# 1/z turned by VectorE, a rearranged beginning and end, ScalarE scaling of the values, and more tiles transposed by DMA in an attention-and-gate kernel

## The chip, the cores and the metric

The kernel runs on one core of a Trainium2 chip. A core has five engines that run their own instruction streams in order: TensorE (PE in the profile; PEld is its loading of weights), VectorE (DVE), ScalarE (ACT), GpSimd (POOL) and SyncE (SP), which here issues every DMA. They wait for one another only by semaphores. SBUF holds the working data, 128 partitions wide; PSUM is the memory that TensorE writes, in eight banks of 512 float32 for each partition. GpSimd does not reach PSUM. The metric is the device time of one execution in microseconds (us), lower being better.

## What is computed

An attention over pooled keys, and then a gated mixture along the rows of its result. Cut to what matters:

```python
# q: (4, 12288, 128), kv: (4, 384, 32, 128), all float32
kv_pool = kv.reshape(B, H // 4, 4, W // 4, 4, C).mean(axis=(2, 4))
k = v = kv_pool.reshape(B, -1, C) @ w_sr          # 768 keys of 128 channels
s = (q @ k.transpose(0, 2, 1)) / np.sqrt(C)
a = np.exp(s - s.max(-1, keepdims=True))
a /= a.sum(-1, keepdims=True) + 1e-09
x = a @ v                                         # (4, 12288, 128)
gate_pre = sum(conv_w[k] * xp[:, k:k + S, :] for k in range(5))   # xp: x behind 4 zero rows
out = (1 / (1 + np.exp(-gate_pre)) * (x @ w_val)) @ w_out
```

`w_val`, `conv_w` and `w_out` come as float64; the kernel takes their words and makes float32 of them on the chip.

## The kernel before

The work is cut into 96 groups of 512 queries, 24 for each of the four batches; a group has four tiles of 128 queries (`NT`), j = 0 to 3. For precision the scores are made of three products of high and low parts (`kh`, `kl`, `qh`, `ql`), and so is the attention's result (`vh`, `vl` with a high and a low float16 half of the probabilities).

A tile goes like this. `score` (L251) makes 128 x 768 scores with six matmuls into a pair of PSUM banks, `s`; there are three such pairs, so the scores of a tile have to wait until the tile three before it has left its pair. `row_max` (L257, VectorE) takes the row's maximum, `expo` (L269, ScalarE) the exponential with the row's sum into a column of `z`, `p_hi` (L316, ScalarE) the high half and `p_lo` (L320, VectorE) the low half, which is the last reader of `s`. The probabilities must be transposed before they can be multiplied with the values. That is done in one of two ways. With `j < g.by_dma` the two halves go to `hl` in SBUF, and DMA transposes (L324) bring them to `pt`, two tiles in one DMA or one tile by itself. Otherwise TensorE turns the tile (`turn`, L299, six transposes against the identity) back into its own bank pair ahead of `p_hi`. `by_dma` is 3, so that tile 3 is turned by TensorE; in the last batch it is 4 in every second group.

A group's later steps follow in later groups: 1/z one group later, the product with the values (`av_part`, L333, 18 matmuls in four portions) and `x` (`g_x`, L350, VectorE) two groups later, the convolution's products and sums (L360, L369, GpSimd, and one product L358 on ScalarE) three groups later, `val`, the gate and `out` (L389, L394, L399, L409) four groups later. The product with `w_val`, the product with `w_out`, the turned z and the setup of keys and values share the one bank `m`.

The order on each engine is written out by hand: `tc.manual_schedule()` keeps the program's order, and the loop over t (L470) issues, for tile t, the scores of tile t + 1, then this tile's steps, then the `p_lo` of tile t - 1. So at j = 0 VectorE takes the maximum of tile 0 and then the low half of tile 3 of the group before; `g_x` stands at the end of j = 3.

1/z: `norm_eps` adds 1e-9 on ScalarE at the group's end; in the next group VectorE takes the reciprocal of the four columns (L276, j = 0), TensorE turns the 128 x 128 tile `z` into `m` (L279), VectorE copies the four rows out (L286, j = 1), a DMA stores them to DRAM (`rd<-r`, L287), and another reads them back into every partition (`rb<-rd`, L292, j = 3).

Keys of the next batch are loaded in 16 pieces (`kvt`, L117), one step in each group; VectorE pools them (L120), TensorE projects them (L133), ScalarE writes `kh` and `vt`, VectorE `kl`. `column_scale` finds a power of two for each channel of the values in six small steps (`trickle`, two in each iteration) and makes `diag`, the identity times it; `values` (L176) multiplies `vt` with `diag`, which turns and scales the values at once.

The beginning (L434 to L461) loads and pools the first batch's keys in 16 pieces, projects them in halves and makes the first scores. The 14 small VectorE steps that make float32 of the weights (L89, L93, L96) drip into the first groups. The end (L539 to L592) finishes the last five groups, n5 to n1.

## Time and profile before

| | us |
|---|---|
| median of three runs (their range) | 1077.52 (1075.18 to 1078.14) |
| the profiled execution's own time | 1078.68 |
| its span in the trace | 1076.9 |
| busy in the span: PE, VectorE, ScalarE, GpSimd | 1038.4, 919.5, 903.7, 865.2 |
| span before the first row maximum | 28.25 |
| span behind the last group's sum of z | 26.5 |

The profile is that of one execution. Its page gives the busy time of each engine, a row of digits for each engine along the span, the chain of work that ended last, followed back from the last instruction, and the costliest groups of instructions. The timeline gives instructions of an engine in order of time, neighbours of one kind merged ("x2"), with the idle time before them in brackets and what ended it. TensorE's matmuls are pipelined and their ends are modelled, so starts are to be compared, not ends. "Frame" below means the time from one group's `norm_eps` (L273) to the next one's.

### The profile page before, as it was taken

Reading aid. Unit: us, or ns where it says so; the run is one execution under the profiler, and the core shown is the slowest. Engines: PE = TensorE matmul, PEld = TensorE weight load, DVE = VectorE, ACT = ScalarE, POOL = GpSimd, SP = SyncE. Lnnn points to the kernel's source line nnn. Section 1 sums busy time; section 2 is a strip of 40 time slices with the busy share of each in tenths; the row PEclk is TensorE's granted clock in tenths of the full one; section 3 lists DMA queues with packets and bytes.
Section 4 is the critical chain, followed back from the end, with each engine's and each line's share of the span. In section 5 each row is a group of like instructions: output and inputs, shape, how many; then the busy total and the mean of one; then the engine's idle time right before and its main releaser. Section 6 shows DMA issues by size and latency. Waiting matters only on the chain.

```text
span 1076.9 us, 16475 instructions
## 1 busy us (share of the span) xinstructions
PE 1038.4 (96%) x5102; PEld 706.5 (66%) x5102; DVE 919.5 (85%) x1290; ACT 903.7 (84%) x1659; POOL 865.2 (80%) x948
## 2 busy tenths in 40 slices
PE   1899999999999999999999999999999999999996
PEld 0666666666666666666676666666666666666663
DVE  6888989898888898988888989898888888888885
ACT  1788888888888888888888888888888988888882
POOL 0178888888888888888888888888887888888882
PEclk9999999999999999999999999999999999999999
DMA  7699999998889999999689999997899999999994
GB/s 285 115 237 215 214 225 234 200 192 190 182 186 234 226 222 224 220 214 188 156 182 221 248 216 219 235 218 177 174 203 191 200 209 218 206 194 212 201 178 120
DMA packets 505527, 220.25 MB, mean 205 GB/s; under 512 B 471520, under 2 KB 472288, under 8 KB 505440
## 3 DMA queue, kind: packets, MB, share of 16 engines
q1 hardware_dynamic: 505440, 219.20, 92.7%
q8 instruction: 41, 0.67, 0.2%
q14 instruction: 46, 0.38, 0.1%
HBM read 75.83 MB, written 25.36 MB: 94 GB/s over the span
## 4 chain that ended last, share of the span: by engine, by line
PE 89%; DVE 5%; ACT 2%; DMA 2%; issue 1%; POOL 0%; SPq 0%; DVEq 0%; ACTq 0%
PE s L251 36%; PE av L333 32%; PE m L389 7%; PE m L399 7%; PE s L299 5%; DMA kvt<-in_kv 2%; DVE nm L257 1%; PE m L279 1%; ACT s L269 1%; ACT hl L316 1%; DVE hl L320 1%; DVE pt L320 1%; DVE pool L120 0%; DVE x L350 0%; PE m L176 0%
## 5 line engine op out<-in xcount | busy, mean ns | idle before, releaser
L333 PE MATMUL av<-pt,vh 128*128 128x512 f16 x1140 | 387.1, 381 | 0.0
L369 POOL TENSOR_TENSOR sum<-sum,tap 128x512 f32<-128x512 f32 x282 | 360.3, 1278 | 22.1
L257 DVE TENSOR_REDUCE nm<-s 128x1 f32<-128x768 f32 x384 | 363.9, 948 | 2.8 <-PE s L251 2.8
L269 ACT ACTIVATE s<-s,nm 128x768 f32<-128x768 f32 x300 | 262.0, 873 | 88.7 <-DVE nm L257 80.0
L360 POOL TENSOR_SCALAR tap<-x,wm 128x512 f32<-128x512 f32 x376 | 253.4, 693 | 78.1 <-DVE x L350 76.8
L320 DVE SCALAR_TENSOR_TENSOR hl<-s,hl 128x768 f16<-128x768 f32 x300 | 284.8, 949 | 21.4 <-ACT hl L316 21.1
L251 PE MATMUL s<-kh,qh 128*128 128x384 f32 x768 | 252.9, 410 | 6.0 <-DVE hl L320 2.3
L316 ACT ACTIVATE hl<-s 128x768 f16<-128x768 f32 x300 | 243.0, 810 | 9.1
L333 PEld LDWEIGHTS <-vh 128*128 128x128 f16 x1164 | 113.5, 98 | 173.6 <-issue 81.5
L333 PE MATMUL av<-pt,vl 128*128 128x512 f16 x570 | 216.0, 379 | 0.0
L251 PE MATMUL s<-kh,ql 128*128 128x384 f32 x768 | 198.0, 339 | 0.0
L251 PE MATMUL s<-kl,qh 128*128 128x384 f32 x768 | 197.7, 338 | 0.0
L237 POOL TENSOR_TENSOR ql<-q,qh 128x512 fp32r<-128x512 f32 x96 | 122.0, 1271 | 93.3 <-ACT qh L233 92.5
L251 PEld LDWEIGHTS s<-kh,qh 128*128 128x128 f32 x768 | 132.4, 192 | 51.1 <-PE m L279 4.4
L251 PEld LDWEIGHTS s<-kl,qh 128*128 128x128 f32 x768 | 140.5, 189 | 0.5 <-DVE kl L146 0.5
L251 PEld LDWEIGHTS s<-kh,ql 128*128 128x128 f32 x768 | 139.8, 189 | 0.0
L394 DVE SCALAR_TENSOR_TENSOR h<-th,m 128x512 f32<-128x512 f32 x94 | 64.7, 688 | 69.0 <-PE m L389 63.4
L369 POOL TENSOR_TENSOR sum<-tap,tap 128x512 f32<-128x512 f32 x94 | 120.3, 1280 | 0.0
L350 DVE SCALAR_TENSOR_TENSOR x<-av,down,rb 128x512 f32<-128x512 f32 x95 | 71.3, 751 | 44.5 <-POOL ql L237 30.5
L333 PEld LDWEIGHTS <-vl 128*128 128x128 f16 x582 | 57.2, 98 | 76.6 <-issue 53.6
L399 PE MATMUL m<-h,wm 128*128 128x512 f32 x188 | 96.8, 597 | 1.2 <-DVE h L394 1.2
L389 PE MATMUL m<-x,wm 128*128 128x512 f32 x188 | 96.1, 592 | 0.0
(68 smaller groups left out, 1001.9 us busy)
## 6 DMA issues: line engine op xcount, KB each, us to landing
kvt<-in_kv SPq DMA_DIRECT2D x64, 384.0 KB
rb<-rd SPq DMA_DIRECT2D x96, 256.0 KB
q<-in_q SPq DMA_DIRECT2D x47, 512.0 KB
out<-o SPq DMA_DIRECT2D x46, 512.0 KB
pt<-hl SPq DMA_TRANSPOSE x192
rd<-r SPq DMA_DIRECT2D x96, 2.0 KB
out<-o SPq DMA_DIRECT2D x3, 256.0 KB
q<-in_q SPq DMA_DIRECT2D x2, 256.0 KB
```

The costliest lines, as they stand in the source:

```text
L237: nc.gpsimd.tensor_tensor(out=g.ql, in0=g.q, in1=g.qh.bitcast(F32), op=ALU.subtract)
L251: nc.tensor.matmul(s[:, h, :HALF], a[:, sl], k[:, h * HALF:(h + 1) * HALF], start=(i == 0), stop=(i == 2))
L257: nc.vector.tensor_reduce(out=nm, in_=g.s[j], axis=AX.XY, op=ALU.max, negate=True)
L269: nc.scalar.activation(out=halves(g.pf[j]) if on_pe(g, j) else g.s[j], in_=g.s[j], func=AF.Exp, bias=g.nm.pop(j), accum_out=g.z[:, j:j + 1])
L316: nc.scalar.activation(out=part(g, j, 0), in_=g.s[j], func=AF.Copy, scale=2.0 ** 15)
L320: nc.vector.scalar_tensor_tensor(out=part(g, j, 1), in0=g.s.pop(j), scalar=2.0 ** 15, in1=part(g, j, 0), op0=ALU.mult, op1=ALU.subtract)
L333: nc.tensor.matmul(out, g.st[v][:, k * P:(k + 1) * P], g.pt[:, j0:j1, a * NCH + k], start=(i == 0), stop=(i == len(AV_ORDER) - 1))
L350: nc.vector.scalar_tensor_tensor(out=g.x[:, HALO + c0:HALO + c1], in0=av, scalar=g.st["down"], in1=g.rb[:, c0:c1], op0=ALU.mult, op1=ALU.mult)
L360: eng.tensor_scalar(out=g.tap[k], in0=src, scalar1=w, scalar2=1.0, op0=ALU.mult, op1=ALU.mult)
L369: nc.gpsimd.tensor_tensor(out=s, in0=acc, in1=g.tap[k], op=ALU.add)
L389: nc.tensor.matmul(m, wval, g.x[:, HALO + c0:HALO + c1], start=True, stop=True)
L399: nc.tensor.matmul(m, wout, h, start=True, stop=True)
```

## The change

The parts, by what they do:

- 1/z: the reciprocal moves behind the low half of tile 3. VectorE then turns `z`, now 128 x 32, in four 32 x 32 transposes, and the store is issued there, still at j = 0. TensorE's transpose of `z` and VectorE's copy out of `m` are gone. `norm_rows`, the read back, moves from the end of j = 3 to j = 2.
- Transposes: tile 3 goes by DMA (`by_dma` 4) in every second group of the last batch, as before, and in the first three batches in groups 0, 18, 20 and 22, which load no keys: 12 groups more.
- Values: ScalarE scales `vt` in place by a column of powers of two, and `values` only transposes it against the identity. The VectorE step that made `diag` is gone.
- Beginning: the weights are loaded first, and their 14 VectorE steps run there; GpSimd pools six of the 16 pieces in four halvings each; the keys are projected in pieces of 384, 288 and 96 columns; the scores of the first three tiles are made in two halves, the first of them ahead of the last pieces.
- End: the products for n2 and n1 stand one behind the other, the last groups' convolutions have two of five products on ScalarE (`conv_mixed` in place of `conv_dve`), and the order of the rest is new.

```diff
-    zs = [const.tile([P, P], F32, name=f"z{i}") for i in range(3)]
+    zs = [const.tile([P, BLOCK], F32, name=f"z{i}") for i in range(3)]
...
-            lambda: v.tensor_scalar_mul(out=st["diag"], in0=ident, scalar1=up.bitcast(F32)),
+            lambda: nc.scalar.activation(out=st["vt"], in_=st["vt"], func=AF.Copy,
+                                         scale=up.bitcast(F32)),
...
-            nc.tensor.matmul(m[:, j * P:(j + 1) * P], st["vt"][:, k:k + P], st["diag"],
-                             start=True, stop=True)
+            nc.tensor.transpose(m[:, j * P:(j + 1) * P], st["vt"][:, k:k + P], ident)
...
-    def norm_turn(g, m):
-        nc.tensor.transpose(m[:, :P], g.z, ident)
-        g.rm = m[:NT, :P]
+    def norm_turn(g):
+        g.r = small.tile([BLOCK, P], F32, name="r")
+        for i in range(0, P, BLOCK):
+            nc.vector.transpose(out=g.r[:, i:i + BLOCK], in_=g.z[i:i + BLOCK])
...
-            g.by_dma = 4 if b == B - 1 and i % 2 == 0 else 3
+            g.by_dma = 4 if i % 2 == 0 and (b == B - 1 or not 0 < i <= PIECES + 1) else 3
...
+    convert = load_moe()
     for i in range(AHEAD):
         load_kv(0, st, i)
...
+    by_pool = (1, 3, 5, 7, 9, 11)
+    ends = {PIECES // 2: slice(0, HALF), PIECES - 2: slice(HALF, NK - 2 * PC),
+            PIECES: slice(NK - 2 * PC, NK)}
+    for step in convert:
+        step()
+    for i in range(1, PIECES + 1):
+        if i - 1 + AHEAD < PIECES:
+            load_kv(0, st, i - 1 + AHEAD)
+        (pool_halving if i in by_pool else pool_kv)(st, i - 1)
...
+        if i == PIECES - 3:
+            for j in first:
+                score(at(0), j, (0,))
...
-            score(nxt, (j + 1) % NT)
+            score(nxt, (j + 1) % NT, (1,) if t + 1 in first else range(2))
...
-        if last and j == 0:
-            norm_reciprocal(last)
-        if last and j == 1:
-            norm_store(last)
+        if last and j == 2:
+            norm_rows(last)
         drip()
         if prev:
             p_lo(prev, (j - 1) % NT)
...
         if last and j == 0:
-            norm_turn(last, misc())
+            norm_reciprocal(last)
+            norm_turn(last)
+            norm_store(last)
...
-        if last and j == 3:
-            norm_rows(last)
...
+    for i in range(NT):
+        av_part(n2, i)
...
+    avs = pair_of(half)
+    av_range(n1, avs[0], 0, len(AV_ORDER), 0, NT // 2)
     n4.m = g_val(n4, misc())
+    av_range(n1, avs[1], 0, len(AV_ORDER), NT // 2, NT)
     new_x(n2, n3, nc.scalar.copy)
     g_x(n2, n2.av)
+    gate2 = conv_mixed(n2, 0, GQ)
...
+    g_x(n1, avs[0], *cuts[0])
     h4 = g_h(n4.th, n4.m)
...
+    gates = [conv_mixed(n1, *cuts[0])]
...
+    g_x(n1, avs[1], *cuts[1])
...
+    gates.append(conv_mixed(n1, *cuts[1]))
```

What the change moves on an engine is best seen where the streams themselves are listed, by line, operation and tiles (the numbers at the names tell buffers of one name apart). First VectorE in one group of the first batch, from `x` to `h`. Before:

```order
L350 SCALAR_TENSOR_TENSOR x_1481<-av_1366,down_214,rb_1355 128x512
L257 TENSOR_REDUCE nm_1503<-s_1451 128x1
L276 RECIPROCAL z1_102<-z1_102 128x4
L320 SCALAR_TENSOR_TENSOR pt_1445<-s_1428,pt_1445 128x768
L257 TENSOR_REDUCE nm_1525<-s_1488 128x1
L286 COPY r_1531<-m_1512 4x128
L320 SCALAR_TENSOR_TENSOR hl_1506<-s_1451,hl_1506 128x768
L394 SCALAR_TENSOR_TENSOR h_1536<-th_1508,m_1521 128x512
```

The same stretch after the change:

```order
L363 SCALAR_TENSOR_TENSOR x_1652<-av_1538,down_273,rb_1487 128x512
L270 TENSOR_REDUCE nm_1672<-s_1623 128x1
L333 SCALAR_TENSOR_TENSOR pt_1617<-s_1598,pt_1617 128x768
L289 RECIPROCAL z2_103<-z2_103 128x4
L295 STREAM_TRANSPOSE r_1681<-z2_103 32x32 x4
L270 TENSOR_REDUCE nm_1700<-s_1657 128x1
L333 SCALAR_TENSOR_TENSOR hl_1675<-s_1623,hl_1675 128x768
L418 SCALAR_TENSOR_TENSOR h_1707<-th_1677,m_1696 128x512
```

The low half of tile 3 (`pt<-s,pt`) stands one place earlier, the reciprocal behind it, and four transposes come between it and the maximum of tile 1; the copy ahead of the low half of tile 0 (`hl<-s,hl`) is gone.

Second SyncE's queue over two groups of the last batch, the first with seven tiles' worth of transposes between two stores of 1/z. Before:

```order
L324 DMA_TRANSPOSE pt_11049<-hl_10981 128x24x128
L287 DMA rd_11126<-r_11125 4x128
L324 DMA_TRANSPOSE pt_11165<-hl_11099 128x24x128
L324 DMA_TRANSPOSE pt_11165<-hl_11099 128x12x128
L292 DMA rb_11202<-rd_11126 128x512
L413 DMA out_0<-o_11072 128x1024
L287 DMA rd_11249<-r_11248 4x128
```

After:

```order
L337 DMA_TRANSPOSE pt_11090<-hl_11019 128x24x128 x2
L300 DMA rd_11150<-r_11145 4x128
L305 DMA rb_11204<-rd_11150 128x512
L337 DMA_TRANSPOSE pt_11207<-hl_11138 128x24x128
L337 DMA_TRANSPOSE pt_11207<-hl_11138 128x12x128
L300 DMA rd_11273<-r_11268 4x128
L437 DMA out_0<-o_11113 128x1024
```

The read back `rb<-rd` now stands right behind the store that it reads, and ahead of the next group's transposes instead of behind them.

Third ScalarE in group 22 of the first batch, after the change (before, the same stretch has no operation on `vt`):

```order
L282 ACTIVATE s_2957,z1_102<-s_2957,nm_3009 128x2x384
L329 ACTIVATE hl_2941<-s_2957 128x768
L180 ACTIVATE vt_511<-vt_511,up_2921 128x768
L245 CAST qh_3020<-q_2739 128x512
L282 ACTIVATE s_2997,z1_102<-s_2997,nm_3037 128x2x384
```

The scaling of all 768 columns of `vt` comes between the high half of tile 2 and the exponential of tile 3.

## Rows read from the trace of the kernel before

**Rows 1.** From the page: the busy time of each engine with its share of the span and its instructions, and the share of each engine in the chain that ended last.

```profile
PE 1038.4 (96%) x5102; PEld 706.5 (66%) x5102; DVE 919.5 (85%) x1290; ACT 903.7 (84%) x1659; POOL 865.2 (80%) x948
...
PE 89%; DVE 5%; ACT 2%; DMA 2%; issue 1%; POOL 0%; SPq 0%; DVEq 0%; ACTq 0%
```

**Rows 2.** The timeline of ScalarE at the `norm_eps` of some groups: start, duration, instruction. In order: groups 19, 21, 23, 24 and 25 (the first batch's end and the second's beginning), then 78, 79 and 80 of the last batch.

```profile
237.13 0.21 ACT L273 ACTIVATE z<-z 128x4 f32<-128x4 f32 x1
...
259.69 0.21 ACT L273 ACTIVATE z<-z 128x4 f32<-128x4 f32 x1
...
281.62 0.20 ACT L273 ACTIVATE z<-z 128x4 f32<-128x4 f32 x1
...
292.23 0.21 ACT L273 ACTIVATE z<-z 128x4 f32<-128x4 f32 x1
...
303.55 0.20 ACT L273 ACTIVATE z<-z 128x4 f32<-128x4 f32 x1
...
873.20 0.20 ACT L273 ACTIVATE z<-z 128x4 f32<-128x4 f32 x1
...
883.49 0.20 ACT L273 ACTIVATE z<-z 128x4 f32<-128x4 f32 x1
...
894.10 0.20 ACT L273 ACTIVATE z<-z 128x4 f32<-128x4 f32 x1
```

**Rows 3.** The timeline of TensorE in the frame behind group 79, whose tile 3 it turns itself: the six transposes, the end of a portion of `av`, the transpose of z, the scores of the next tile; then the end of another portion and the scores behind it.

```profile
883.66 0.82 PE L299 MATMUL s<-ident,pf 128*128 128x128 f32 x6
...
886.46 0.59 PE L333 MATMUL av<-pt,vh 128*128 128x512 f16 x2
886.89 0.27 PE L279 MATMUL m<-ident,z 128*128 128x128 f32 x1
...
887.35 0.51 PE L251 MATMUL s<-kl,qh 128*128 128x384 f32 x2
...
889.13 0.38 PE L333 MATMUL av<-pt,vh 128*128 128x512 f16 x1
...
889.70 0.51 PE L251 MATMUL s<-kl,qh 128*128 128x384 f32 x2
```

**Rows 4.** The timeline of VectorE in the same frame; in brackets the idle time before an instruction and what ended it.

```profile
883.93 0.75 DVE L350 SCALAR_TENSOR_TENSOR x<-av,down,rb 128x512 f32<-128x512 f32 x1 [0.88 <-POOL ql L237]
...
885.46 0.17 DVE L276 RECIPROCAL z<-z 128x4 f32<-128x4 f32 x1
885.54 0.93 DVE L320 SCALAR_TENSOR_TENSOR pt<-s,pt 128x768 f16<-128x768 f32 x1
886.39 0.95 DVE L257 TENSOR_REDUCE nm<-s 128x1 f32<-128x768 f32 x1
887.25 0.27 DVE L286 COPY r<-m 4x128 f32<-4x128 f32 x1
887.45 0.95 DVE L320 SCALAR_TENSOR_TENSOR hl<-s,hl 128x768 f16<-128x768 f32 x1
```

**Rows 5.** The timeline in the frame behind group 78, whose tile 3 went by DMA: the low half of tile 3 on VectorE, the idle time of TensorE's weight load (PEld) and the scores behind it.

```profile
875.25 0.93 DVE L320 SCALAR_TENSOR_TENSOR hl<-s,hl 128x768 f16<-128x768 f32 x1
...
876.29 0.30 PEld L251 LDWEIGHTS s<-kh,qh 128*128 128x128 f32 x2 [0.40 <-PE m L279]
...
876.75 0.34 PE L251 MATMUL s<-kl,qh 128*128 128x384 f32 x1
```

**Rows 6.** Groups of instructions by line and shape: count, busy us, mean ns of one, idle time before them.

```profile
L176 PE MATMUL m<-diag,vt 128*128 128x128 f32 x48 | 6.9, 280 | 0.4 <-ACT o L409 0.4
...
L188 DVE TENSOR_TENSOR vl<-m,vh 128x384 f16<-128x384 f32 x8 | 4.4, 546 | 0.0
```

**Rows 7.** The timeline of VectorE in the frame behind group 21, where the steps of the column scale drip in: a step on one column, and the next maximum.

```profile
263.44 0.14 DVE L164 TENSOR_SCALAR pw<-big 128x1 int32<-128x1 int32 x1
263.50 0.95 DVE L257 TENSOR_REDUCE nm<-s 128x1 f32<-128x768 f32 x1
```

**Rows 8.** The timeline of ScalarE later in the same frame: an operation on 128 x 768 out of PSUM into SBUF.

```profile
269.81 0.91 ACT L269 ACTIVATE pf<-s,nm 128x768 f32<-128x768 f32 x1
```

**Rows 9.** The timeline of the beginning: the last piece's pooling, the second half's projection, the first row maximum.

```profile
22.67 0.95 DVE L120 TENSOR_REDUCE pool<-kvt 128x48 f32<-128x768 f32 x1 [0.80 <-DMA kvt<-in_kv]
23.68 1.65 PE L133 MATMUL s<-pool,wsr 128*128 128x384 f32 x2 [7.82 <-DVE pool L120]
...
28.25 0.96 DVE L257 TENSOR_REDUCE nm<-s 128x1 f32<-128x768 f32 x1 [1.42 <-PE s L251]
```

**Rows 10.** The timeline of the end: the read back of 1/z for the last group but one, the store of the last, the last product with the values for the last group but one, the last read back, `x` of the last group but one, a chain of four dependent steps of its convolution, the last `h`.

```profile
1053.73 0.84 SPq L292 DMA_DIRECT2D rb<-rd  x1
...
1054.63 0.32 SPq L287 DMA_DIRECT2D rd<-r  x1
...
1054.93 0.38 PE L333 MATMUL av<-pt,vh 128*128 128x512 f16 x1
...
1057.19 0.32 SPq L292 DMA_DIRECT2D rb<-rd  x1
1058.01 0.75 DVE L350 SCALAR_TENSOR_TENSOR x<-av,down,rb 128x512 f32<-128x512 f32 x1 [4.73 <-POOL sum L369]
...
1059.79 3.11 DVE L377 SCALAR_TENSOR_TENSOR fast<-x,wm,fast 128x512 f32<-128x512 f32 x4
...
1072.53 0.42 DVE L394 SCALAR_TENSOR_TENSOR h<-th,s 128x256 f32<-128x256 f32 x1 [0.15 <-ACT th L385]
```

More of the change, by code (lines that the diff above doesn't have):

```diff
@@ L18 @@
 GQ = 512
+BLOCK = 32
 NT = GQ // P
@@ L122, in pool_kv, with pool_halving @@
                                 axis=AX.X, op=ALU.add)
+    def pool_halving(st, i):
+        t = st.pop(("kv", i)).rearrange("c (k s) -> c k s", s=RR)
+        n = RR // 2
+        while n:
+            if n == 1:
+                to = st["pool"][:, i * PC:(i + 1) * PC].rearrange("c (k s) -> c k s", s=1)
+            else:
+                to = kvp.tile([C, PC, n], F32, name=f"half{n}", bufs=1)
+            nc.gpsimd.tensor_tensor(out=to, in0=t[:, :, :n], in1=t[:, :, n:2 * n], op=ALU.add)
+            t, n = to, n // 2
     def key_tiles(st):
@@ L211, in setup_steps @@
         steps = [lambda i=i: piece(i) for i in range(PIECES + 1)]
-        steps += [lambda h=h: project(st, h, misc()) or split_keys(st, h) for h in range(2)]
+        steps += [lambda sl=sl: project(st, sl, misc()) or split_keys(st, sl)
+                  for sl in (slice(0, HALF), slice(HALF, NK))]
         return steps + value_steps(st)
@@ L371, in g_conv, with conv_mixed, product @@
         g.gate = acc
-    def conv_dve(g, c0=0, c1=GQ):
+    def conv_mixed(g, c0, c1):
+        def product(k):
+            t = work.tile([C, GQ], F32, name=f"tap{k}", bufs=1 if k < TAPS - 1 else 2)
+            t = t[:, :c1 - c0]
+            nc.scalar.activation(out=t, in_=g.x[:, k + c0:k + c1], func=AF.Copy,
+                                 scale=cwt[:, k:k + 1])
+            return t
+        late = [product(k) for k in range(TAPS - 2, TAPS)]
         s = work.tile([C, GQ], F32, name="fast")[:, :c1 - c0]
         nc.vector.tensor_scalar_mul(out=s, in0=g.x[:, c0:c1], scalar1=cwt[:, 0:1])
-        for k in range(1, TAPS):
+        for k in range(1, TAPS - 2):
             nc.vector.scalar_tensor_tensor(out=s, in0=g.x[:, k + c0:k + c1],
@@ L379, in conv_dve @@
                                            op0=ALU.mult, op1=ALU.add)
+        for t in late:
+            nc.vector.tensor_tensor(out=s, in0=s, in1=t, op=ALU.add)
         return s
@@ L439, in attn_moe_kernel @@
     nc.sync.dma_start(out=wsr, in_=w_sr)
-    g_qh(at(0))
-    g_ql(at(0))
+    first = range(3)
+    by_pool = (1, 3, 5, 7, 9, 11)
+    ends = {PIECES // 2: slice(0, HALF), PIECES - 2: slice(HALF, NK - 2 * PC),
+            PIECES: slice(NK - 2 * PC, NK)}
     low = None
-    for i in range(PIECES):
-        if i + AHEAD < PIECES:
-            load_kv(0, st, i + AHEAD)
-        if i == 3:
-            convert = load_moe()
-        pool_kv(st, i)
-        if i == 3 * PIECES // 4:
+    for step in convert:
[4 more added lines that the diff above has]
+        (pool_halving if i in by_pool else pool_kv)(st, i - 1)
+        if i == PIECES // 2:
+            g_qh(at(0))
+            g_ql(at(0))
+        if low and (i == PIECES - 1 or i == PIECES - 3):
             low()
-        if i % (PIECES // 2) == PIECES // 2 - 1:
-            h = 2 * i // PIECES
-            project(st, h, bank_pair()[:, 0])
-            high, low = split_keys(st, h)
+            low = None
+        if i in ends:
+            project(st, ends[i], misc())
+            high, low = split_keys(st, ends[i])
             high()
+        if i == PIECES - 3:
+            for j in first:
+                score(at(0), j, (0,))
     low()
@@ L458, in attn_moe_kernel @@
     load_pair(at(2), at(3))
-    score(at(0), 0)
+    score(at(0), 0, (1,))
     g_qh(at(1))
```

83 lines of the change are left out of this document (35 added, 48 removed).

## The prediction

> **What bounds the kernel now.** I read the page first, then the frames between groups, then TensorE and VectorE inside a frame, then the two ends. TensorE is busy for 96% of the span and is 89% of the chain that ended last [rows 1], so in the middle a TensorE instruction less is time less, as long as nothing else is nearly as late. The frames say how near that is. Behind group 79, whose tile 3 TensorE turns itself, a frame takes 894.10 - 883.49 = 10.61 us; behind group 78, whose tile 3 went by DMA, it takes 10.29 [rows 2]. The six transposes hold TensorE for about 0.64 us (six at a pitch of 0.11, [rows 3]), but only 0.32 came back. Why is seen one step further: the low half of tile 3 ends at 876.18, TensorE's weight load sits idle for 0.40 us and starts 0.11 after that end [rows 5]. The page puts this idle time down to TensorE's own z transpose, but the bank pair's last reader is the low half, so I take VectorE as the releaser. So a closed loop lies right behind TensorE: `av` ends, VectorE makes `x`, the maximum of tile 0, the low half of tile 3, the maximum of tile 1, the low half of tile 0, and only then is a bank pair free for the scores of tile 3. The change takes work from TensorE and puts some on this loop, so the question is which of the two ends last.
>
> **1/z, TensorE's side.** From the last `av` start (886.46 plus a pitch of 0.21) to the `kl` scores it is 0.68 us with the z transpose between them and 0.57 without [rows 3]. TensorE saves 0.11 in each frame; a frame that it alone bounds falls from 10.61 to 10.50.
>
> **1/z, VectorE's side.** I lay the new order into the frame behind group 79 [rows 4]. The low half of tile 3 takes the reciprocal's place and runs from 885.46 to 886.39. Independent instructions overlap by 0.08 (the maximum at 886.39 starts before the low half ends at 886.47), so the reciprocal runs from 886.31 to 886.48. The four transposes of 32 x 32 are new, and no row shows one. From below: a step on one column adds only 0.06 between two large ones (263.44 to 263.50, [rows 7]), with 31 columns more about 0.10. From above: the copy of 128 columns took 0.27 [rows 4]. The nearest row is the one-column step, 0.14; between it and the maximum of 768 columns, 0.95, a column costs about 0.0011, so 32 columns are about 0.17. I take them one behind the other, since each has another group of partitions as input and they share the unit's transposing path, with the 0.03 that dependent steps show (four of 0.75 in 3.11 us, [rows 10]): a pitch of 0.20. That ends them at 886.50 + 3 x 0.20 + 0.17 = 887.27. The maximum of tile 1 then runs from 887.19 to 888.14 and the low half of tile 0 from 888.16 to 889.11; it ends now at 888.40. TensorE's `kl` scores for tile 3 stand at 889.70 and could stand at 889.59 without the z transpose. They follow the end of the low half by 0.57 behind group 78 [rows 5], and by 0.51 where VectorE is less crowded, so they come at 889.62 to 889.68: 0.03 to 0.09 late. **The frame becomes 10.50 + 0.05 = 10.55**, bound by VectorE, whether tile 3 goes by DMA or not. What was cover is used up: 0.70 us more on the loop, against some 0.65 that it had to spare.
>
> The Trainium skill (VectorE: DVE Perf Modes, Two Vector instructions with no wait between them) states that an instruction whose input starts in another group of 32 partitions than the last one's is held until all earlier ones have finished. No run here shows it; by it the four transposes are serial as I take them, and the overlapped case below falls away.
>
> **The store and the read back.** The store has its data at about 887.3 instead of 887.5. The read back now waits for it in SyncE's queue, with the next tiles' transposes behind it. How long that is shows at the end, where nothing else is queued: the last store's issue is over at 1054.95 and its read back starts at 1057.19, 2.2 us later [rows 10]. In most groups the store now has the time until the next transposes are ready; behind a group that goes all by DMA it is issued late, and delays the next transposes by those 2.2 us. Their product with the values is two groups away, so I cost it at nothing. If that cover were gone, each such group would pay up to 2.2 us.
>
> **More tiles by DMA.** In 12 frames TensorE loses 0.64 us, but VectorE's loop is the same 10.55, so they gain what the others gain. For the 11 such frames of the last batch, now 10.29, the loop is a loss of 0.26 each.
>
> **The sum of the middle.** 53 regular frames of the first three batches: 53 x -0.06 = -3.2. Two project frames a batch, now 11.28 each (237.13 to 259.69, [rows 2]): TensorE 11.17 in the first; in the second, whose tile goes by DMA, VectorE's 10.55 + 0.46 (one more split on 384 columns, 0.55 less the overlap, [rows 6]) = 11.01; together 3 x (-0.11 - 0.27) = -1.1. Two frames with `values`, now 11.32 (292.23 to 303.55): three of the six passes go (48 passes in 24 products now, [rows 6]), which leaves TensorE 10.88 and VectorE 11.01: 6 x -0.31 = -1.9. The two frames in which the column scale drips in, now 21.93 together (259.69 to 281.62): the maximum over `vt` and the transposes stand in the same loop, +0.25, and ScalarE's scaling of 768 columns, for which I take 0.91 [rows 8], delays the exponential of tile 3 and so its low half by another +0.27; 3 x 0.52 = +1.6. Last batch: 11 x 0.26 + 10 x -0.06 = +2.3. Middle: **-2.3 us**.
>
> **The beginning.** From the last pooling to the first maximum it is 28.25 - 22.67 = 5.6 us [rows 9]. With 96 columns instead of 384 in the last projection (1.65 us) and its three evacuations, and half the scores, I get about 3.4: -2.2. ScalarE is the slower engine in the first three groups, and the scaling of `vt` (0.91) and the transposed values stand in its way, while the 14 conversion steps leave VectorE; I keep -2.4 at the third group. Against that, the loads wait longer for their buffers: the second piece is pooled only behind the conversion, and a halving on GpSimd is slower than the 0.95 of one pooling. I charge +1.0 for a later last piece. **-1.4**, bounds -4 and +1.
>
> **The end.** `x` of the last group but one waits until 1058.01, 4.73 us idle [rows 10]. Its product is over at 1055.3; what it waits for is the read back that was issued at 1053.73, behind the last transposes. Moved ahead of them it is no longer last, and `x` starts some 2.6 us earlier. The last group's read back, issued at 1057.19, becomes late next: about 1 us later than now, since the transposes come behind the other read back, with its `x` near 1061.5. Behind that VectorE has `x`, `h`, a half convolution, `x`, `h`, the other half and three more `h` (a half convolution of five steps, each a little over half of the 0.78 for 512 columns, is about 2.2 us, an `h` or `x` 0.4 to 0.7), some 8 us in a row, so the last `h` ends near 1069.6 instead of 1072.95. **-3.4**, bounds -1 and -5.
>
> **Sum.** -2.3 - 1.4 - 3.4 = -7.1 against 1078.68 of the profiled execution (1076.9 of span and 1.8 around it): 1071.6. That execution stands 1.2 above the median 1077.52, so **1070 us**.
>
> **Rivals.**
>
> *The transposes overlap.* With a pitch of 0.10 the low half of tile 0 ends by 888.76 and TensorE stays the bound: frames of 10.50, and 10.23 where tile 3 goes by DMA. Regular frames give -0.11 and three of them -0.4, the special ones of the first three batches another -5, the last batch -2: middle -13.5, in all -18.3, or **1059**. For it speaks that VectorE's small steps do overlap [rows 7]; against it that those all start in the same partitions.
>
> *The transposes are slow, and the kernel gets slower.* This is VectorE's loop again, at another price: half-way between 0.17 and the copy's 0.27 a transpose is 0.22, the pitch 0.25, and the low half of tile 0 ends 0.20 later, at 889.31. The frame is 10.76. Some 86 frames hang on the loop, so the sum moves by 86 x 0.21 = +18, to **1088**. It decides from a frame of 10.63, where 86 x 0.08 eats the 7.1; that is a transpose of 0.19. For it speaks that a block must be filled before it can be emptied, against it that no row of so few columns is that long.
>
> The Trainium skill (VectorE: DVE Perf Modes, The three transpose paths) gives 311 ns for VectorE's transpose of 128 x 128 in bf16. Less 96 columns at the slope above, an estimate is 0.21 us; by it the frame is 10.73 and the sum would be about 1085. No run here shows it.
>
> *The ends don't give it.* The later last piece and the later last read back eat the 4.8 us; then 1075.
>
> **How the numbers follow.** The forecast has a chance of 0.43, the overlapped transposes 0.25, the slow ones 0.24, ends without a gain 0.08. The range reaches from below the overlapped case's 1059 into the middle of the slow case: 1057 to 1085. About 0.3%, or 3.2 us, is what a measurement of this kernel can tell from no change. Faster by more: nearly all of the forecast and the overlapped case, 0.62. Within: the forecast's upper edge, the ends without a gain, the mild part of the slow case, 0.21. Slower: the rest of the slow case, 0.17.
>
> **What would show it.** In the profile after: the four transposes' duration and pitch (0.17 and 0.20); regular frames at 10.55 and those of the last batch's all-DMA groups at the same, not 10.29; TensorE idle before the scores of tile 3, released by the low half of tile 0; no z transpose on TensorE. The scaling of `vt` should be followed by a late exponential in three frames. The first maximum should come near 26.5 us, `x` of the last group but one right behind its product. Frames of 10.50 with the transposes overlapping would prove the first rival, frames above 10.63 the second. If transposes by DMA land late and TensorE waits for `pt`, I have mispriced the queue.

## The result, and the profile after

The changed kernel takes 1084.78 us (median of four runs, 1083.59 to 1085.35), the kernel before beside it 1077.83; the ratio is 1.0066 with a 95% interval of 1.005 to 1.0082. It is slower by about 7 us where I had forecast a gain of 7. The profiled execution took 1083.59 us with a span of 1081.8.

From the page: busy time and the chain that ended last, which answer to [rows 1].

```profile
PE 1032.1 (95%) x4912; PEld 682.3 (63%) x4912; DVE 973.8 (90%) x1569; ACT 920.4 (85%) x1671; POOL 879.4 (81%) x972
...
DVE 33%; PE 28%; ACT 27%; POOL 8%; issue 4%; DMA 1%; SPq 0%; ACTq 0%; DVEq 0%; POOLq 0%
DVE nm L270 12%; PE s L265 12%; ACT s L282 11%; PE av L346 10%; ACT hl L329 9%; POOL ql L249 6%; DVE x L363 5%; DVE r L295 5%; DVE pt L333 4%; DVE hl L333 3%; ACT tap L371 3%; ACT qh L245 3%; PE m L423 3%; PE m L413 2%; PE s L312 1%
```

TensorE went from 89% of the chain to 28%. It no longer bounds the kernel by itself; a loop through VectorE, ScalarE and GpSimd does, and the transposes (`DVE r`) are 5% of the chain. The timeline of ScalarE at the `norm_eps` of groups 78, 79 and 80 gives the frames that [rows 2] gave:

```profile
875.62 0.21 ACT L286 ACTIVATE z<-z 128x4 f32<-128x4 f32 x1
886.23 0.20 ACT L286 ACTIVATE z<-z 128x4 f32<-128x4 f32 x1
896.89 0.21 ACT L286 ACTIVATE z<-z 128x4 f32<-128x4 f32 x1
```

Behind group 78 (all by DMA) a frame takes 10.61, where it took 10.29; behind group 79 it takes 10.66, where it took 10.61. Regular frames of the first three batches stand at 10.60. The cause is read in the same frame behind group 78, on VectorE and then on TensorE's weight load; they answer to [rows 4, 5].

```profile
876.14 0.75 DVE L363 SCALAR_TENSOR_TENSOR x<-av,down,rb 128x512 f32<-128x512 f32 x1 [0.96 <-POOL ql L249]
876.80 0.95 DVE L270 TENSOR_REDUCE nm<-s 128x1 f32<-128x768 f32 x1
877.67 0.95 DVE L333 SCALAR_TENSOR_TENSOR hl<-s,hl 128x768 f16<-128x768 f32 x1
878.53 0.17 DVE L289 RECIPROCAL z<-z 128x4 f32<-128x4 f32 x1
878.73 0.84 DVE L295 STREAM_TRANSPOSE r<-z 32x32 f32<-32x32 f32 x4
879.51 0.90 DVE L270 TENSOR_REDUCE nm<-s 128x1 f32<-128x768 f32 x1
880.45 0.96 DVE L333 SCALAR_TENSOR_TENSOR hl<-s,hl 128x768 f16<-128x768 f32 x1
```

```profile
881.52 0.30 PEld L265 LDWEIGHTS s<-kh,qh 128*128 128x128 f32 x2 [0.67 <-PE m L413]
```

The four transposes hold VectorE for 0.84 us (0.20 each, a pitch of 0.21). The low half of tile 0 therefore ends at 881.41, and the weights of the next scores are loaded 0.11 later, after 0.67 of idle time. The profile puts this idle time down to TensorE's own `m`, as it did in [rows 5]; that the low half is the releaser is read from the 0.11, and turn_none and look below bear it out.

By stretches, from the same view of both kernels: to the first `norm_eps` +1.26 us, the three frames behind it +1.0, the 92 frames of the rest +3.24, behind the last `norm_eps` -0.59 (25.95 for 26.54); together the span's 4.9. The beginning on VectorE, for [rows 9]:

```profile
21.97 1.90 DVE L121 TENSOR_REDUCE pool<-kvt 128x48 f32<-128x768 f32 x2 [0.56 <-DMA kvt<-in_kv]
26.13 0.46 DVE L158 SCALAR_TENSOR_TENSOR kl<-m,kh 128x288 fp32r<-128x288 f32 x1 [2.27 <-ACT vt L155]
26.51 0.94 DVE L121 TENSOR_REDUCE pool<-kvt 128x48 f32<-128x768 f32 x1
...
30.06 1.92 DVE L270 TENSOR_REDUCE nm<-s 128x1 f32<-128x768 f32 x2 [1.10 <-PE s L265]
```

The last pooling stands behind the low part of 288 columns, which waits 2.27 us; the first maximum comes at 30.06 instead of 28.25. The end on VectorE, and GpSimd's sums beside it, for [rows 10]:

```profile
1060.84 0.75 DVE L363 SCALAR_TENSOR_TENSOR x<-av,down,rb 128x512 f32<-128x512 f32 x1 [1.29 <-POOL sum L382]
...
1062.41 3.32 DVE L399 SCALAR_TENSOR_TENSOR fast<-x,wm,fast 128x512 f32<-128x512 f32 x2
1065.83 1.49 DVE L403 TENSOR_TENSOR fast<-fast,tap 128x512 f32<-128x512 f32 x2
1067.24 0.48 DVE L363 SCALAR_TENSOR_TENSOR x<-s,down,rb 128x256 f32<-128x256 f32 x1
...
1076.35 0.75 DVE L418 SCALAR_TENSOR_TENSOR h<-th,s 128x256 f32<-128x256 f32 x2 [1.73 <-PE s L413]
```

```profile
1060.82 4.36 POOL L382 TENSOR_TENSOR sum<-sum,tap 128x512 f32<-128x512 f32 x3
```

`x` of the last group but one does start right behind its product, but two steps of its convolution take 3.32 us together, where four such took 3.11 in [rows 10], and the last `h` waits 1.73 for TensorE.

### The profile page after: what moved, and what is told of

Read it like the earlier page. It is cut to its first block, busy times and chain, and to the rows that moved or that the text cites. A ratio compares the mean times of both kernels' runs of the same rounds, so it can differ in the third digit from the quotient of the medians.

```text
span 1081.8 us, 16241 instructions
## 1 busy us (share of the span) xinstructions
PE 1032.1 (95%) x4912; PEld 682.3 (63%) x4912; DVE 973.8 (90%) x1569; ACT 920.4 (85%) x1671; POOL 879.4 (81%) x972
## 4 chain that ended last, share of the span: by engine, by line
DVE 33%; PE 28%; ACT 27%; POOL 8%; issue 4%; DMA 1%; SPq 0%; ACTq 0%; DVEq 0%; POOLq 0%
DVE nm L270 12%; PE s L265 12%; ACT s L282 11%; PE av L346 10%; ACT hl L329 9%; POOL ql L249 6%; DVE x L363 5%; DVE r L295 5%; DVE pt L333 4%; DVE hl L333 3%; ACT tap L371 3%; ACT qh L245 3%; PE m L423 3%; PE m L413 2%; PE s L312 1%
## 5 line engine op out<-in xcount | busy, mean ns | idle before, releaser
L270 DVE TENSOR_REDUCE nm<-s 128x1 f32<-128x768 f32 x384 | 359.9, 937 | 1.7 <-PE s L265 1.6
L282 ACT ACTIVATE s<-s,nm 128x768 f32<-128x768 f32 x312 | 273.3, 876 | 76.5 <-DVE nm L270 70.6
L333 DVE SCALAR_TENSOR_TENSOR hl<-s,hl 128x768 f16<-128x768 f32 x312 | 297.5, 953 | 26.1 <-ACT hl L329 22.9
L329 ACT ACTIVATE hl<-s 128x768 f16<-128x768 f32 x312 | 252.9, 811 | 9.1
L329 ACT ACTIVATE pt<-s 128x768 f16<-128x768 f32 x72 | 58.4, 812 | 30.7 <-PE s L312 30.7
```

What stands on the lines that cost most here:

```text
L270: nc.vector.tensor_reduce(out=nm, in_=g.s[j], axis=AX.XY, op=ALU.max, negate=True)
L282: nc.scalar.activation(out=halves(g.pf[j]) if on_pe(g, j) else g.s[j], in_=g.s[j], func=AF.Exp, bias=g.nm.pop(j), accum_out=g.z[:, j:j + 1])
L329: nc.scalar.activation(out=part(g, j, 0), in_=g.s[j], func=AF.Copy, scale=2.0 ** 15)
L333: nc.vector.scalar_tensor_tensor(out=part(g, j, 1), in0=g.s.pop(j), scalar=2.0 ** 15, in1=part(g, j, 0), op0=ALU.mult, op1=ALU.subtract)
```

## The experiments

Ratios are to the kernel before, run on the same chip; there it took 1077.05 to 1077.94 us, so a difference of two medians from different chips is good to about 1 us. The changed kernel's ratio is 1.0066.

| kernel | median, us | ratio (95% interval) |
|---|---|---|
| turn_alone | 1081.84 | 1.0041 (1.0028 to 1.0054) |
| turn_old | 1078.59 | 1.0011 (1.0002 to 1.002) |
| turn_late | 1102.98 | 1.024 (1.0216 to 1.0265) |
| dma_old | 1086.59 | 1.0088 (1.0074 to 1.0102) |
| turn_gap | 1114.7 | 1.0344 (1.033 to 1.0358) |
| turn_none | 1067.27 | 0.9902 (0.9889 to 0.9916) |
| ends_old | 1081.44 | 1.0035 (1.0022 to 1.0047) |
| block | 1070.38 | 0.9932 (0.9919 to 0.9946) |
| block_alone | 1066.14 | 0.9901 (0.9887 to 0.9916) |
| block_end | 1069.06 | 0.9923 (0.9909 to 0.9938) |
| best | 1068.49 | 0.9914 (0.99 to 0.9927) |
| block_ends_old | 1063.44 | 0.9875 (0.9862 to 0.9889) |
| block_dma_old | 1071.35 | 0.9947 (0.9935 to 0.996) |
| block_ends_dma_old | 1067.56 | 0.9913 (0.9899 to 0.9926) |
| block_rows_late | 1064.02 | 0.9877 (0.9862 to 0.9892) |
| block_begin_old | 1066.82 | 0.9898 (0.9879 to 0.9917) |
| block_end_old | 1067.8 | 0.9905 (0.9888 to 0.9923) |

My theory: the transposes stand in VectorE's loop and set the frame. The rival: 1/z costs nothing there and the loss lies at the beginning and the end.

**turn_alone and turn_old: 1/z by itself, and all but 1/z.**

> The kernel before with the new 1/z alone (reciprocal, four VectorE transposes and store behind the low half of tile 3, read back at j = 2). Loop theory (the transposes stand in VectorE's loop, which then sets every frame): the 11 all-DMA frames of the last batch go from 10.29 to 10.60 us, regular frames stay at 10.60 to 10.61 although TensorE has 0.11 less to do; +3.4 in the middle, about -2 at the end because the read back for the last group but one is issued earlier, so about 1079 us. Rival (1/z costs nothing in the middle; beginning and end of the change make it slower): all-DMA frames stay at or below 10.29, regular ones fall to 10.50; 1070 us or less.

> The changed kernel with the 1/z of before (TensorE turns z, VectorE copies the rows out, store at j = 1, read back at j = 3), all other parts of the change kept. Loop theory: all-DMA frames return to 10.29 (11 of the last batch, and some of the 12 new ones), regular ones stay at 10.61; -3.4 in the last batch, about -2 elsewhere, up to +2 at the end from the later read back: 1080 to 1082 us. Rival: frames unchanged, 1085 to 1087 us.

In turn_alone the all-DMA frames went to 10.60 to 10.62, the others of the last batch from 10.61 to 10.67, regular ones stayed at 10.60 to 10.62; it was 2.8 us slower than expected, since the three frames behind the first group, where VectorE also has the conversion, took 33.68 in place of 30.31. In turn_old the all-DMA frames were 10.28 to 10.29 again, but for two of the last batch, and the time fell by 0.55%, 6 us. The rival falls: 1/z carries most of the loss. What is left in turn_old is not faster than before either.

**turn_none: the price of the transposes.**

```diff
-        g.r = small.tile([BLOCK, P], F32, name="r")
-        for i in range(0, P, BLOCK):
-            nc.vector.transpose(out=g.r[:, i:i + BLOCK], in_=g.z[i:i + BLOCK])
+        g.r = ident
```

> The changed kernel without the four transposes: the reciprocal and the store stay in their places, but rows of the identity are stored, so 1/z does not reach the output. It shows what is left when VectorE is spared 0.84 us. If TensorE does gain 0.11 in each frame without its own turn of z: regular frames 10.50, all-DMA frames 10.2, 1070 to 1073 us. If 10.60 has another cause than the transposes: regular frames stay at 10.60, only all-DMA frames fall to 10.29, 1079 to 1081 us.

ScalarE's `norm_eps` of groups 78 to 80 in turn_none:

```profile
863.95 0.21 ACT L286 ACTIVATE z<-z 128x4 f32<-128x4 f32 x1
874.17 0.21 ACT L286 ACTIVATE z<-z 128x4 f32<-128x4 f32 x1
884.66 0.21 ACT L286 ACTIVATE z<-z 128x4 f32<-128x4 f32 x1
```

Frames of 10.22 and 10.49: TensorE does gain 0.11 from the z transpose that is gone, and the four transposes cost all of it and more: 17.5 us in the kernel. The edit also frees the store from waiting for the reciprocal; look, below, keeps that wait and has the same frames.

**turn_late and turn_gap: another place.**

```diff
-        if last and j == 0:
+        if last and j == 1:
             norm_reciprocal(last)
```

> The changed kernel with the reciprocal, the transposes and the store moved from behind the low half of tile 3 (j = 0) to behind the low half of tile 0 (j = 1), out of the stretch that ends with a free bank pair; before the change VectorE stood idle for 0.80 us there. Loop theory: the loop is shorter by 1.0 us, TensorE is the bound again, regular frames 10.50 and all-DMA frames 10.2 to 10.3, about -14 us: 1071 us. Rival (the transposes cost by VectorE's total work, or the loss lies at the beginning and the end): frames stay at 10.6, 1083 to 1086 us.

The timeline of VectorE in the frame behind group 78 of turn_late:

```profile
896.69 0.96 DVE L333 SCALAR_TENSOR_TENSOR hl<-s,hl 128x768 f16<-128x768 f32 x1 [0.23 <-ACT hl L329]
897.57 0.17 DVE L289 RECIPROCAL z<-z 128x4 f32<-128x4 f32 x1
897.77 0.84 DVE L295 STREAM_TRANSPOSE r<-z 32x32 f32<-32x32 f32 x4
898.64 0.69 DVE L418 SCALAR_TENSOR_TENSOR h<-th,m 128x512 f32<-128x512 f32 x1
```

The same `h` in turn_none, with the idle time ahead of it:

```profile
869.25 0.69 DVE L416 SCALAR_TENSOR_TENSOR h<-th,m 128x512 f32<-128x512 f32 x1 [0.34 <-PE m L411]
```

Both theories missed. `h` starts 5.88 us into this frame (892.76 is its `norm_eps`), in turn_none 5.30, and the frame is 10.79 against 10.22: what `h` is late by, the frame is long by. Without the transposes VectorE was idle ahead of `h` for 0.34 there (0.67 in frames whose tile TensorE turns), and 1/z takes about 0.95. So neither place that was tried is outside the loop; each has a slack of its own, and the place that I chose has less than the old one (regular frames of 10.73 against 10.60). Beyond that, single frames of 11 to 12 us stand where key pieces are loaded; in the longest of the second and of the third batch TensorE waits 1.22 and 1.64 us for `pt`.

```diff
+        if last and j == 0:
+            last.late = not pooling and gi < G - 1
+        if last and j == (NT - 1 if last.late else 0):
             norm_reciprocal(last)
...
+        if avg and avg.late and j == 0:
+            norm_rows(avg)
```

> The changed kernel with the reciprocal, the four transposes and the store at j = 3, ahead of x, in groups in which VectorE pools no key piece (there it stood idle for about 1.0 us ahead of x); in groups that pool a piece they stay at j = 0. The read back of such a group then comes at j = 0 of the next one. If what costs is that they stand between the maximum of tile 0 and the free bank pair: the last batch gets its all-DMA frames back (10.29 in place of 10.60) and its other frames go to 10.5 or 10.6, 3.4 to 5 us in the last batch, 1079 to 1081 us in all. If any place on VectorE costs the same, since what it does later only moves x: no frame below 10.55, 1083 to 1087 us.

Both missed again, for another reason. SyncE's queue in turn_gap, and TensorE in the same stretch of the last batch:

```profile
962.95 0.43 SPq L300 DMA_DIRECT2D rd<-r  x1
965.12 0.33 SPq L305 DMA_DIRECT2D rb<-rd  x1
965.54 10.70 SPq L337 DMA_TRANSPOSE pt<-hl  x3
```

```profile
973.14 0.61 PE L346 MATMUL av<-pt,vh 128*128 128x512 f16 x1 [2.41 <-DMA pt<-hl]
```

The read back is issued 2.2 us after the store, waits for it at the head of the queue, and the next transposes stand behind it until 965.54; issuing three of them then takes 10.70 us. TensorE waits 2.41 us for `pt`. The frames of the last batch go up to 14.7 us. The cover that I had relied on for the queue (the product is two groups away) is thin in such groups. How much of the lateness is the read back's wait and how much the transposes' own time in the queue was not separated.

**dma_old: the 12 new all-DMA groups.**

```diff
-            g.by_dma = 4 if i % 2 == 0 and (b == B - 1 or not 0 < i <= PIECES + 1) else 3
+            g.by_dma = 4 if b == B - 1 and i % 2 == 0 else 3
```

> The changed kernel with tile 3 by DMA only in every second group of the last batch, as before (12 groups fewer). Loop theory: no difference, since VectorE's loop sets the frame whether TensorE turns tile 3 or not, 1084 to 1086 us. Rival one (TensorE is the bound): 12 frames longer by 0.3, 1088 us. Rival two (the transposes of these groups crowd SyncE's queue): faster, 1081 us or less.

Group 18 of a batch has a frame of 10.60 to 10.61 either way, as the loop theory says. The median is just above its range; the interval overlaps that of the changed kernel, so whether it is slower can't be told.

**look: why four transposes take 0.84 us.**

```diff
-            nc.vector.transpose(out=g.r[:, i:i + BLOCK], in_=g.z[i:i + BLOCK])
+            nc.vector.transpose(out=g.r[:, i:i + BLOCK], in_=g.z[:BLOCK])
...
-    tap(n3, TAPS - 1, nc.scalar)
-    g_conv(n3)
+    n3.gate = n3.x[:, :GQ]
```

> Two things left out or changed in the changed kernel, far apart in the trace. All four transposes read the first 32 partitions, so that 1/z is wrong for the other rows; and at the end the convolution of the last group but two is left out (its gate is a copy of x), so that GpSimd is idle there. First: if an instruction is held because its input begins in another group of partitions, the pitch of the four falls from 0.21 to 0.17 or less; if transposes are one behind the other in any case, it stays at 0.21. Second: if VectorE's steps of 1.64 us in the convolution of the last group but one are long because GpSimd adds at the same time, they take 0.75 us; if it is their own form, 1.64 again.

VectorE in the frame behind group 78 of look, and at its end:

```profile
866.84 0.17 DVE L289 RECIPROCAL z<-z 128x4 f32<-128x4 f32 x1
867.05 0.48 DVE L295 STREAM_TRANSPOSE r<-z 32x32 f32<-32x32 f32 x4
867.46 0.90 DVE L270 TENSOR_REDUCE nm<-s 128x1 f32<-128x768 f32 x1
868.29 0.94 DVE L333 SCALAR_TENSOR_TENSOR hl<-s,hl 128x768 f16<-128x768 f32 x1
```

```profile
1044.72 0.75 DVE L363 SCALAR_TENSOR_TENSOR x<-av,down,rb 128x512 f32<-128x512 f32 x1 [1.60 <-issue]
...
1046.11 1.54 DVE L399 SCALAR_TENSOR_TENSOR fast<-x,wm,fast 128x512 f32<-128x512 f32 x2
...
1051.00 0.48 DVE L363 SCALAR_TENSOR_TENSOR x<-s,down,rb 128x256 f32<-128x256 f32 x1 [1.76 <-DMA rb<-rd]
```

The same four instructions, all from partitions 0 to 31, take 0.48 together, a pitch of 0.09 and 0.156 each behind the first, and the frames are 10.22 and 10.49, as with no transposes. One run gave 1067.39. What was dear is that each starts in another group of 32 partitions than the one ahead of it: such transposes don't overlap (0.20 each at a pitch of 0.21), those of look do. One step more is late with them: in the changed kernel the low half of tile 0, which reads `hl` from partition 0 on, starts 0.04 behind the end of the maximum ahead of it (880.45), in look 0.07 before that end (868.29). The Trainium skill (VectorE: DVE Perf Modes, Two Vector instructions with no wait between them) says that such an instruction starts only when all earlier ones have finished; the trace agrees.

At the end, without GpSimd's sums, the two steps took 1.54 together in place of 3.32. The Trainium skill (SBUF — State Buffer, SBUF: two separate sides) states that a VectorE instruction with two SBUF inputs and a GpSimd instruction that reads SBUF exclude each other; the rows agree as far as they go: 3.32 beside GpSimd's adds, 1.54 without them. But the tail was 25.81, hardly shorter: the next `x` now waits 1.76 for the last read back, and starts 11.2 us behind the last `norm_eps` (1039.79).

**ends_old: beginning and end as before.** The diff's parts for both are undone, 1/z keeps its new form.

> The changed kernel with the beginning and the end of before (conversion in the first groups, all pooling on VectorE, projections of 384 columns, whole scores, the old order of the end with its convolution on VectorE alone); 1/z, values and the DMA groups as changed. If the new beginning costs what the traces show (1.3 to the first sum of z and 1.0 in the three frames behind it): 2 us earlier at the fourth group. At the end the old order now has the read back for the last group but one early, and its convolution runs behind GpSimd's sums: tail 24 to 26 us against 25.95. In all 1081 to 1083 us. If beginning and end are worth what I forecast (-1.4 and -3.4), it is slower instead: 1087 to 1090 us.

0.31% less than the changed kernel, 3.3 us; the tail is 24.53. The new beginning and end cost time, they don't save it. In the traces of the eleven kernels with the changed beginning the first maximum lies between 30.06 and 33.11, in those of the eight with the old one between 27.00 and 28.39; the 1.8 us between the two profiled executions above is near the least that it costs there.

**block and block_alone: one instruction in place of four.**

```diff
-                             func=AF.Exp, bias=g.nm.pop(j), accum_out=g.z[:, j:j + 1])
+                             func=AF.Exp, bias=g.nm.pop(j), accum_out=g.z[:, j * BLOCK:j * BLOCK + 1])
...
-        for i in range(0, P, BLOCK):
-            nc.vector.transpose(out=g.r[:, i:i + BLOCK], in_=g.z[i:i + BLOCK])
+        nc.vector.transpose(out=g.r, in_=g.z)
...
-        nc.sync.dma_start(out=g.rd, in_=g.r[:NT])
+        nc.sync.dma_start(out=g.rd.rearrange("j (b q) -> b j q", q=BLOCK),
+                          in_=g.r[::BLOCK].rearrange("b (j q) -> b j q", q=BLOCK))
```

> The changed kernel with one transpose of 128 x 128 in place of four of 32 x 32: the four sums of z stand 32 columns apart, one VectorE instruction turns all blocks where they are, and the store takes partitions 0, 32, 64 and 96. Nothing starts in another group of partitions. Hold theory (the four small transposes were dear because each waits for the one ahead of it to finish, not because transposing is dear): the instruction takes about 0.3 us by the 0.0011 a column seen before, the frames are 10.49 and 10.22 as without any transpose, 1067 to 1069 us. Rival (a transpose pays per block, whatever its neighbours): 16 blocks, 0.8 us or more, frames of 10.6 or longer, 1083 us or more.

> The kernel before with 1/z turned by that one VectorE instruction and nothing else of the change. Hold theory: regular frames 10.50, all-DMA frames 10.22, about -7 us in the middle and -2 at the end (read back earlier): 1067 to 1070 us. If it comes out at the time of the kernel above, the change's other parts are worth nothing together. Rival (TensorE's turn of z was free in the kernel before): 1076 to 1079 us.

VectorE in the frame behind group 78 of block:

```profile
870.70 0.17 DVE L289 RECIPROCAL z<-z 128x4 f32<-128x4 f32 x1
870.90 0.32 DVE L294 STREAM_TRANSPOSE r<-z 128x128 f32<-128x128 f32 x1
871.14 0.92 DVE L270 TENSOR_REDUCE nm<-s 128x1 f32<-128x768 f32 x1
```

0.32 us for sixteen blocks, and the next maximum overlaps it. The frames are 10.49 and 10.22. block is 14 us faster than the changed kernel, block_alone 16 us faster than turn_alone, which differs from it in nothing else. With look, in whose frames only the start partitions differ, this shows the cause: four instructions that each start in another group of partitions. block_alone also beats block: in the change, what is not 1/z costs 3 to 4 us.

**block_end and best: mending the end and the beginning.**

```diff
-    g_out(g_h(n3.th, m3), o3)
     g_val(n1, ms[1], *cuts[1])
+    g_out(g_h(n3.th, m3), o3)
...
-    for th, m, o, c in zip(ths, ms, pair_of(half), cuts):
+    for th, m, o, c in zip(ths, ms, (misc()[:, :half], last_bank[:, :half]), cuts):
```

> The one-instruction kernel with two things moved in the new end: the second half product with w_val for the last group stands ahead of the product with w_out for the last group but two, and the last two products with w_out go to two banks of their own and not to two halves of one tile. If these two waits (1.73 us ahead of the last h, 0.6 to 0.8 between the last two evacuations) are the end's loss, the tail falls by 1.5 to 2.3 us and the time with it. If another wait stands right behind them, by less than 0.5.

> The same, and in the beginning the weights are loaded behind the first pieces, two of the 14 conversion steps run behind each pooling from the seventh on, the low part of 288 columns stands behind the last pooling, and the last projection has a bank of its own. If the beginning's loss is the late loads and the 2.3 us that the last pooling waits behind the low part: first maximum at 27 to 28 us in place of 30, 1.5 to 2.5 us less in all, the fastest of all runs. If the loads' own pace sets it: within 0.5 us of the kernel above.

The tail fell from 26.18 to 24.32, as expected, and the median by 1.3, with intervals that overlap. best missed: it was only 0.6 faster than that, which can't be told from nothing, and its first maximum came at 31.94, within the range of the changed beginning. The last two pieces' loads were issued at 19.65 and 22.03 us, in the kernel before at 16.80 and 17.76. They wait for a buffer, and six of 16 pieces are pooled by GpSimd in about 2.4 us each where VectorE takes 0.95. But in best VectorE itself is late too: the first conversion step holds it for the weights, loaded later there, and from then until the last pooling ends at 29.3 it is not idle.

```profile
16.48 0.92 DVE L90 TENSOR_SCALAR rest<-raw 128x261 int32<-128x261 int32 x1 [4.34 <-DMA raw<-in_w_moe]
```

Which of these is the beginning's loss stays open; no run kept all else and gave VectorE the pieces, or took the conversion alone out of the beginning.

**The other parts, one by one, with the one instruction.** Each of these is block with parts of the change undone.

> The changed kernel with the one-instruction 1/z and with the beginning and the end of before. If beginning and end are worth less than nothing, as they were with four transposes: 1066 to 1068 us, level with the kernel before with the one instruction (1066.1). If the other 4 us lie in the all-DMA groups or in the values: 1069 to 1071 us.

> The changed kernel with the one-instruction 1/z and with tile 3 by DMA only in the last batch's groups, as before. TensorE is the bound now, so by the frames (10.49 against 10.22) each of the 12 groups loses 0.27, 3 us in all, unless late transposes ate that: 1073 us if the groups give what their frames say, 1070 if what they give is eaten elsewhere, 1068 if the late transposes (frames of 11 to 12 us) come from them.

> Both undone: what is left of the change is the one-instruction 1/z and the scaling of the values by ScalarE. Against the kernel before with the one instruction (1066.1) this tells the values alone: six frames 0.37 shorter, three pairs of scale frames 0.1 to 0.5 longer by the traces so far, so 1064 to 1066 us. If ScalarE's scaling delays more than that: 1067 us or more.

> The first of these four with the read back of 1/z at j = 3 as before, behind the next transposes in SyncE's queue, not ahead of them. If the read back, waiting for its store, holds the transposes behind it: no frames of 11 to 12 us with TensorE waiting for pt in the middle, and 1 to 3 us less there; at the end x of the last group but one is later, up to 2 us more. If the transposes are late for another reason: the same frames, and 1 to 2 us slower in all.

> The changed kernel with the one-instruction 1/z and the beginning of before, the end as changed. If the new beginning is what costs, with the late frames in the middle as its consequence: 1065 us, no frames of 11 to 12 us, a tail of 26. If the late frames come by chance in any run: they are here too, 1068 us.

> The same with the end of before and the beginning as changed. If the beginning costs and the late frames go with it: a tail of 24.5, late frames as before, 1068 to 1069 us. If the end is the larger part: 1066 us or less.

With both old ends the kernel takes 1063.44 us, 1.25% (1.11% to 1.38%) less than before: the fastest of all. Its chain, from the page, is TensorE's again:

```profile
PE 73%; DVE 12%; ACT 9%; POOL 2%; DMA 2%; issue 1%; SPq 0%; DVEq 0%; ACTq 0%
```

By the ratios that is 6 us less than block; the old beginning alone gives 3.7 of them, the old end alone 2.9, though its interval overlaps block's. The 12 all-DMA groups are worth 4.1 us here (1067.56 without them), where neither the changed kernel (dma_old) nor block (block_dma_old, 1071.35) gained from them anything that can be told. The values give nothing that can be told (1067.56 against block_alone's 1066.14, intervals overlapping): their frames are 0.38 shorter (11.19 to 10.81), but the first of the two scale frames is 0.82 longer and the second 0.42 shorter. The read back at j = 3 changes nothing in the middle and lengthens the tail from 24.45 to 26.42. Regular frames that grew to 11 to 12 us, in part with TensorE waiting for `pt`, appeared in block, block_end, best, block_begin_old and block_end_old. They did not in block_ends_old and block_rows_late, which have both old ends, nor in block_dma_old, block_ends_dma_old and block_alone, which lack the 12 groups. So in these traces they take the 12 groups and a new beginning or end together; each trace is one execution, and beginning and end don't change the loop, so why they come and go is open.

## Why the prediction was wrong

The sum was -7.1 us and the profiled span grew by 4.9. Of the 12.0 between them 5.5 lie in the middle, 3.6 at the beginning and 2.8 at the end.

- **TensorE saves 0.11, 10.50 without VectorE's load:** right (turn_none, 10.49).
- **The loop as the next bound, serial transposes, the same frame with tile 3 by DMA or not:** right in kind, though the chain from the page also runs through ScalarE's exponentials and GpSimd's `ql`, which I had not laid out. The step that failed is the price of the transposes: the term "0.17, pitch 0.20" was undersized: 0.20 and 0.21, and 0.03 behind the reciprocal. The row that I took as nearest, a step on one column, could not show it. The frame became 10.60, not 10.55: 53 x 0.05 = +2.7 us on the regular frames and about +1.5 in the last batch. The time went the way of the rival of slow transposes, which decided at 0.19, but not by its reason: one instruction turned sixteen blocks in 0.32 (block), and regular frames stayed under its sign of 10.63.
- **The overlapping rival** was rejected because of the start partitions, and that reason was the right one: where they are equal, its frames of 10.50 and 10.23 came true (look). The other half of my reason, a shared transposing path, is not borne out: in look four transposes overlap.
- **The estimate of 0.21 us for a transpose, a frame of 10.73 and 1085 us:** the time came to 1084.78 by luck. Regular frames were 10.60, and more than half of the miss lies at the two ends, which that estimate left as forecast.
- **The small terms:** project frames gained 0.3 where I had 1.1, values 1.5 for 1.9, scale frames cost 1.7 for 1.6. With the above the middle is +3.24 instead of -2.3.
- **The beginning, -1.4:** failed in sign, +2.25. From the last pooling to the first maximum it fell by 2.0, as forecast (2.2). The step that failed is the charge of +1.0 "for a later last piece": the last pooling came 3.84 later (26.51 for 22.67), behind a wait of 2.27 for the low part of 288 columns that was not in my sum at all. That six slow poolings on GpSimd made the rest is argued, not shown.
- **The end, -3.4:** `x` came 2.67 earlier in the tail, as forecast, and the first `x` of the last group 11.4 us behind the last `norm_eps`, where I had 11.1; VectorE's slow steps hid the last read back there, and without them it set the 11.2 of look. The step that failed is "some 8 us in a row" behind that `x`, with no wait for TensorE in it: it was 9.9, of which 1.73 is the last `h` waiting for TensorE. From the end of that `h` to the end of the span it took another 0.75 more than before. block_end, which moves both, shortened the tail by 1.86. The tail gained 0.59. So the rival of ends that give nothing (0.08) came true as well: +1.7 in place of -4.8.
- **The queue at nothing:** held in the changed kernel (TensorE's weight load waited for `pt` twice, 0.6 us in all); turn_gap showed how little more it bears.

## What to carry to other kernels

Four small VectorE transposes overlapped where all start in the same group of partitions, and ran one behind the other where each starts in another; when one step must touch all groups, look for a layout in which a single wide instruction does it. Where a loop stands close behind the bound, a step moved onto it costs its length less the slack of that one place, so read the idle time just behind the place and not the engine's busy share. A part that saves time on an engine is worth that only while the engine is the bound and nothing else is late: the same 12 groups gave nothing that could be told in two kernels and 4 us in a third.

## What the runs showed of the hardware

- Four 32 x 32 float32 transposes on VectorE took 0.84 us from four groups of partitions, 0.48 from one; one of 128 x 128, which turns sixteen blocks where they stand, took 0.32.
- A VectorE step with two SBUF inputs on 128 x 512 took 0.75 us with GpSimd idle and 1.64 to 1.65 while GpSimd added.
